# A readiness margin for the TensorE groups of one stage's routing, in a kernel ordered by a list scheduler

## The chip, the core and the metric

The kernel runs on one core of a Trainium2 chip. The core has a matmul engine (TensorE, PE in the profile, with its weight loads as PEld), a vector engine (VectorE, DVE), an activation engine (ScalarE, ACT), GpSimd (POOL) and SyncE (SP), which starts most of the DMAs. Each runs its own stream of instructions in the order in which the program lists them, and they wait for each other through semaphores. The metric is the device time of one execution in microseconds, lower is better.

## What is computed

Two layers over `x` of 8 batches x 2496 rows x 256 columns. The first is a mixing layer in the frequency domain; the second a mixture of 8 experts in which each token goes to one expert of limited capacity.

```python
X = np.fft.rfft(x, axis=1)                    # along the 2496 rows
Yr = Xr @ w_r - Xi @ w_i + b_r                # soft-thresholded by 0.01, as is
Yi = Xr @ w_i + Xi @ w_r + b_i
y = np.fft.irfft(Y, n=x.shape[1], axis=1)     # -> 19968 tokens x 256

logits = y @ w_gate                           # 8 experts, cap = 19968 / 8
order = np.argsort(-flat)                     # greedy: best (token, expert) first,
...                                           # an expert closes when it has cap tokens
h = np.maximum(y[mask] @ w1[e], 0.0)          # 256 -> 1024 -> 256, per expert
out[mask] = h @ w2[e]
```

## The kernel before, in words

**The mixing stage** (`phase_a`, some 550 us) goes through the 8 batches as a pipeline. The transform is split as 39 x 64: a short transform of each chunk of `x` (L1120, or L1124 for the last batches), a pass through DRAM that turns the layout, the 64-point transform (L1186), the product with the mixing weights (L1205, twelve 128x256 matmuls per half), the way back (L1221), DRAM again, and the last short transform (L1252, or L1256 for the later batches), whose result `yst` goes to DRAM. fp32 operands are split into a rounded high part and a rest, and multiplied in several passes; the splits keep VectorE, ScalarE and GpSimd busy (L1005 and L1008, L1195 to L1198, L1211 to L1213). L1275 transposes `yst`, L1279 to L1282 cut the transposed tile in three (`yTh`, `yr`, `yTl`), and L1293 multiplies it with the gate weights for the logits.

**The early routing** concerns the first four batches only (`EB = 4`, `EN = 512`). When their logits are there, `ranges` and then `Router.early` look, for each expert, for 512 tokens that belong to it whatever the other batches bring, so that the experts can start on them. This is a long chain of small steps on VectorE with tiny TensorE groups between them, laid among the products of batches 5 to 7. `ranges` has two groups (a transpose at L440, a broadcast at L448). `bisect` halves a threshold 8 times; each time `count` compares the 128x78 logits with it in four `scalar_tensor_tensor` instructions (L467), packs the counts (L471, L472), adds them over the partitions by two small matmuls (L477, L478), and VectorE takes the next threshold from that (L515 to L517). Then follow L810, two groups at L818, and eight groups at L832, whose ranks ScalarE reads (L838, L839). The weights of the first experts are brought meanwhile (L623, cast by L630 on ScalarE, rest by L631 on VectorE).

**Who sets the order.** Nothing is written in execution order. Every step is a task with an engine, a duration from a table, a position and its dependencies (`Plan.add`), and `Plan.run` is a list scheduler: it keeps a clock for each engine, computes when each task is ready (`rtime`: the latest end of its inputs, plus a latency for another engine), and emits the task that can start first; on TensorE `beside` also chooses among those that are ready by the form of the matmul before. What the planner emits is the order of each engine's stream on the chip. A task that the planner holds for ready later is emitted later, and so stands behind more of the others.

**Three places that the steps below come back to.** The PSUM tiles `pt` (transposes of L1275, groups of L440, L818 and L832) and `pc` (counts) are slices of one bank, which the profile shows under the name `both`:

```python
if self.both is None: self.both = self.pp.tile([128, 512], F32, name="both", tag="both", bufs=1)
n, o = int(np.prod(shape[1:])), 0 if s == "pt0" else 480
```

The planner treats `pt` and `pc` as two buffers. The program that is built treats `both` as one tile: a matmul that writes either slice waits for all earlier readers of both, which are `yTh` on ScalarE (L1279) and `yr` on VectorE (L1280). Second, the products of L1205 write to the ring `ps3` of two banks, so that a product waits until VectorE has read the last but one (L1213). Third, a cast of expert weights (L630) stands in ScalarE's stream and holds what is behind it until the weights have landed.

Of the kernel before, what the change touches and what calls it, by code (L numbers as in the profile page):

```python
# [103 lines left out]
class Plan:  # L104
# [11 lines left out]
        self.bufs.append(b)  # L116
        return b

    def add(self, eng, dur, pos, emit, reads=(), writes=(), tail=0.0, after=(), uses=(), nbytes=0.0, form='r', slack=None):
        t = Task()  # L120
        t.form, t.slack = form, slack
        t.eng, t.dur, t.pos, t.emit, t.tail, t.nbytes = eng, dur, pos, emit, tail, nbytes
        t.deps, t.writes, t.end = set(after), list(writes), None
        for b in reads:
            t.deps.update(b.writers)
        t.ords = set()
        for b in writes:
            if b.state:
                t.ords.update(b.users)
                b.users, b.writers = [], []  # L130
            b.writers.append(t)
        for b in list(reads) + list(writes) + list(uses):
            b.users.append(t)
        t.id = len(self.tasks)
        self.tasks.append(t)
        return t
# [24 lines left out]
    def run(self):  # L161
# [21 lines left out]
        def rtime(t):  # L183
            r = 0.0
            for d in t.deps:
                r = max(r, d.end + (lat if d.eng != t.eng else self.own.get(t.eng, 0.0)))
            for d in t.ords:
                r = max(r, d.end + (lat if d.eng != t.eng else 0.0))
            return r
        for t in self.tasks:  # L190
            if not left[t]:
                ready.setdefault(t.eng, []).append([0.0, t])
# [48 lines left out]
        while n < len(self.tasks):  # L241
            best = None
            for eng, lst in ready.items():
                f = free.get(eng, 0.0)
                cand, hold = [], self.hold.get(eng, 0.0)
                for item in lst:
                    r = slot(item[1], item[0])
# [14 lines left out]
            t = item[1]  # L262
# [21 lines left out]
            for s in succ.get(t, ()):  # L284
                left[s] -= 1
                if not left[s]:
                    ready.setdefault(s.eng, []).append([rtime(s), s])
# [23 lines left out]
class Kit:  # L311
# [29 lines left out]

    def dram(self, kind, shape): return self.plan.buf(kind, lambda s: self.dp.tile(shape, F32, name=s, tag=s, bufs=1))

    extra, both, pace = 0.0, None, None

    def v(self, n, pos, emit, reads, writes): return self.plan.add('V', 0.068 + n / 960 + self.extra, pos, emit, reads, writes, after=self.pace() if self.pace else ())

    def t(self, dur, pos, emit, reads, writes, tail=0.0, form='b', slack=None): return self.plan.add('T', dur, pos, emit, reads, writes, tail=tail, form=form, slack=slack)

    def dma(self, pos, emit, nbytes, reads, writes, **k): return self.plan.add('SP', 0.65, pos, emit, reads, writes, tail=1.9, nbytes=nbytes, **k)  # L350

# [61 lines left out]
def load_logits(K, H, LG, LGb, b, lo, pos):  # L413
    q, h = b // 2, b % 2
    for t, r, n, w in ((H.ML[64 * h:64 * h + 64, :, JP * q:JP * q + JP], 0, 8, H.b_ML), (None, 8, 16, lo)):
        K.dma(pos, lambda t=t, r=r, n=n: K.nc.sync.dma_start(lo.t[64 * h:64 * h + 64] if t is None else t, LG[b, r:r + n].rearrange("v (p j) -> p v j", j=JP)), 80e3, [LGb[b]], [w])
# [895 lines left out]
def fast(tc, nc, H, x, w_r, w_i, b_ri, w_gate, cD1, cF, cG, cD5, YD, LG, w1, w2, cR, out, spectral=True):  # L1312
# [10 lines left out]
    with ExitStack() as ctx:  # L1323
        K = Kit(tc, nc, ctx, RINGS, GROUPS)
        K.plan.add('P', 0.5, -28, lambda: make_identity(nc, H.idn), [], [H.b_idn])
        if spectral:
            YDb, LGb, first, Ft = phase_a(K, H, x, w_r, w_i, b_ri, w_gate, cD1, cF, cG, cD5, YD, LG)
        else:
            first, Ft, YDb, LGb = K.plan.buf(None, None), None, *[[K.plan.buf(None, None) for _ in range(B)] for _ in range(2)]
        pos0 = lambda b: 10 * b + 21  # L1330
        constants(K, H, cR, 11, [first], Pace(K.marks, 11, 21, 10))
        R, X = Router(K, H, None, cR), Experts(K, H, YD, YDb, w1, w2, out)
        for b in range(8):
            if not b % 2: lo = K.sb("lo", [128, 16, JP])
            load_logits(K, H, LG, LGb, b, lo, pos0(b))
            if b % 2 and b < 7: route_prep(K, H, b // 2, lo, lambda b=b: pos0(b) + 1)
            if b == EB - 1:
                ranges(K, H, pos0(b) + 1)
                K.extra = 0.12
                R.early(Pos(52.5, 78, 128), Ft)  # L1340
                K.extra = 0.0
        R.late()
        base = 1000
        jobs = []
        for e in range(8):
            W = X.load(base - 33.623, e=e)
            X.run(EN, base, W, R.egi, 4 * e, R.egs[e], R.eoi, 4 * e, lambda t, base=base: base - 22 + .1 * t, early=True)
            base += 16
        for i in range(8):
            wi, gi, gs, oi = R.closing(i, Pos(1023.987 + 63.312 * i, (1114.017 if i else 1135.422) + 63.312 * i, 211 if i < 2 else 98), lo)  # L1350
            W = X.load(base - 26.393, wi=wi)
            X.run(CAP - EN, base, W, gi, 0, gs, oi, 0, lambda t, base=base: base + 16 * (t // 4) - 8.936 + .1 * (t % 4))
            base += 62
        K.lay(RINGS, [("sh", 20480)] + [(k, 2048) for k in dict.fromkeys(s[:-1] for s in G2)] + [("xTh", 3072), ("xTl", 3072), ("xt", 4096), ("half", 64), ("FG", 16384), ("wt", 4096), ("fg", 4096)])
        K.v(1, 2000, lambda: K.V.tensor_copy(H.fail, R.last[0].t[0:1, 0:1]), [R.last[0]], [H.b_fail])
        return K.plan.run()
# [208 lines left out]
```

## Time and profile before

| what | value |
|---|---|
| time, median of 3 runs | 1544.82 us (1542.28 to 1545.27) |
| the profiled execution | 1553.47 us |
| its span, first to last instruction | 1551.6 us |
| TensorE busy | 1517.0 us, 98% of the span |
| VectorE busy | 1071.9 us, 69% |
| ScalarE busy | 852.4 us, 55% |
| GpSimd busy | 670.9 us, 43% |
| granted TensorE clock, mean | 0.996 |

The profiled execution takes 8.65 us more than the median of the runs; 1.87 us of its time lie outside the span. Busy shares are means over stages that differ: the mixing stage with the early routing in it, and then the experts. A matmul's end is modelled, so gaps between matmuls say more than the busy share does. The early routing stands between about 380 and 545 us of the span.

### The profile page before, as it was taken

How to read it: one execution, taken by the hardware profiler on the slowest of the kernel's cores; microseconds unless marked ns; L12 is line 12 of the kernel's file. 1: busy time of each engine (PE TensorE's matmuls, PEld its weight loads, DVE VectorE, ACT ScalarE, POOL GpSimd, SP SyncE). 2: the span in 40 equal slices, each digit the busy share in tenths (PEclk: the TensorE clock that was granted, in tenths of full speed). 3: DMA queues.
4: the chain of work that ended last, by engine and by line, in shares of the span. 5: the costliest groups of instructions: out<-in, count | busy, mean ns of one | idle time of the engine just before them, and what ended most of it. 6: DMA issues, size and time to landing. Idle time of an engine off the chain costs nothing.

```text
span 1551.6 us, 31427 instructions
## 1 busy us (share of the span) xinstructions
PE 1517.0 (98%) x10927; PEld 1357.1 (87%) x10927; DVE 1071.9 (69%) x3524; ACT 852.4 (55%) x1870; POOL 670.9 (43%) x889
## 2 busy tenths in 40 slices
PE   8999999999899999999999999999999999999998
PEld 6998989998788977888788998998998989989997
DVE  4676667676985674789989989887777765542321
ACT  3777888787668787444636235344343443643332
POOL 2246566574535445343333434434335344343332
PEclk9999999999999999999999999999999999999999
DMA  8787787877768576433213122121211212211110
GB/s 271 228 268 245 229 256 232 253 243 214 229 191 279 155 221 176 150 128 115 89 43 102 47 74 67 47 89 57 96 35 55 88 53 97 96 46 45 43 48 29
DMA packets 143892, 210.58 MB, mean 136 GB/s; under 512 B 27836, under 2 KB 107660, under 8 KB 143724
## 3 DMA queue, kind: packets, MB, share of 16 engines
q1 hardware_dynamic: 126882, 164.59, 34.0%
q0 software_dynamic: 16640, 43.77, 8.9%
q8 instruction: 88, 1.44, 0.4%
q14 instruction: 80, 0.66, 0.1%
q10 hardware_dynamic: 202, 0.12, 0.0%
HBM read 123.67 MB, written 84.49 MB: 134 GB/s over the span
## 4 chain that ended last, share of the span: by engine, by line
PE 80%; DVE 6%; issue 4%; DMA 4%; ACT 3%; POOL 1%; SPq 0%; another core or an unknown queue 0%; POOLq 0%; ACTq 0%; DVEq 0%
PE ps L709 25%; PE ps L683 19%; PE ps L1205 10%; PE p L683 6%; PE ps L1186 4%; PE ps L1221 3%; PE p L1120 3%; PE ps L668 2%; PE p L1252 2%; PE p L1256 2%; DVE junk L467 1%; PE both L1275 1%; DMA sh<-T 1%; ACT ajunk L554 1%; DMA xt<-in_moe_w_dram 1%
## 5 line engine op out<-in xcount | busy, mean ns | idle before, releaser
L1205 PE MATMUL ps<-wt,xTh 128*128 128x256 f32 x1280 | 241.6, 287 | 1.0 <-DVE cnt L472 0.7
L1205 PEld LDWEIGHTS ps<-wt,xTh 128*128 128x128 f32 x1280 | 199.9, 188 | 15.1 <-issue 7.1
L1008 POOL TENSOR_TENSOR zl<-y,zh 128x512 fp32r<-128x512 f32 x80 | 108.1, 1351 | 164.2 <-ACT zh L1005 152.7
L1205 PE MATMUL ps<-wt,xTl 128*128 128x256 f32 x640 | 178.6, 279 | 0.0
L722 POOL DMA_INDIRECT out_dram<-xTh,li x64 | 66.3, 1036 | 248.8 <-ACT xTh L718 206.2
L467 DVE SCALAR_TENSOR_TENSOR junk<-h_m,st,h_AG 128x156 bf16<-128x156 f32 (+1 forms) x472 | 163.2, 390 | 2.6
L1282 POOL TENSOR_TENSOR yTl<-yr,yTh 128x468 bf16<-128x468 f32 (+1 forms) x88 | 98.5, 1120 | 86.2 <-ACT yTh L1281 70.1
L1205 PEld LDWEIGHTS ps<-wt,xTl 128*128 128x128 f32 x640 | 120.1, 188 | 0.0
L722 POOL DMA_INDIRECT out_dram<-xTl,li x64 | 65.2, 1019 | 93.0 <-ACT xTl L718 74.1
L1186 PE MATMUL ps<-FG,sh 128*128 128x128 f32 x640 | 99.2, 280 | 4.9 <-DMA TB<-s4st 3.7
L718 ACT COPY xTl<-ps 128x256 f32<-128x256 f32 x80 | 29.9, 374 | 126.2 <-PE ps L709 94.1
L1186 PEld LDWEIGHTS ps<-FG,sh 128*128 128x128 f32 x640 | 87.6, 194 | 11.3 <-DMA TB<-s4st 3.8
L709 PE MATMUL ps<-FG,yTh 128*128 128x256 f32 x430 | 95.0, 283 | 0.0
L709 PE MATMUL ps<-FG,y 128*128 128x256 f32 x443 | 94.2, 281 | 0.0
L718 ACT COPY xTh<-ps 128x256 f32<-128x256 f32 x72 | 27.0, 374 | 110.9 <-PE ps L709 86.8
L1008 POOL TENSOR_TENSOR s2l<-s2c,s2h 120x512 fp32r<-120x512 f32 (+2 forms) x60 | 76.6, 1279 | 21.5 <-DVE s2h L1005 18.3
L1211 DVE TENSOR_TENSOR ps<-ps,bt 128x512 f32<-128x512 f32 x80 | 55.4, 693 | 34.1 <-PE ps L1205 32.7
L1008 DVE TENSOR_TENSOR xl<-xt,xh 117x512 fp32r<-117x512 f32 (+1 forms) x66 | 56.8, 871 | 31.2 <-ACT xh L1005 30.1
L709 PE MATMUL ps<-FG,s1st 128*128 128x256 f32 x341 | 73.4, 284 | 0.0
L1196 DVE TENSOR_TENSOR xTl<-ps,xTh 128x512 fp32r<-128x512 f32 x80 | 54.7, 683 | 25.2 <-ACT xTh L1195 25.1
L1213 DVE SCALAR_TENSOR_TENSOR y<-ps,y 128x512 f32<-128x512 f32 x80 | 55.0, 688 | 24.6 <-ACT y L1212 23.7
L709 PEld LDWEIGHTS ps<-FG,yTh 128*128 128x128 f32 x430 | 70.6, 188 | 1.6
(757 smaller groups left out, 5084.4 us busy)
## 6 DMA issues: line engine op xcount, KB each, us to landing
xt<-in_moe_w_dram SPq DMA_DIRECT2D x64, 512.0 KB
T<-s4st SPq DMA_DIRECT2D x80, 256.0 KB
s2c<-T SPq DMA_DIRECT2D x80, 240.0 KB
YD<-yst SPq DMA_DIRECT2D x80, 234.0 KB
xt<-in_x_dram SPq DMA_DIRECT2D x35, 512.0 KB
sh<-T SPq DMA_DIRECT2D x35, 512.0 KB
T<-s1st SPq DMA_DIRECT2D x70, 240.0 KB
sh<-in_x_dram SPq DMA_DIRECT2D x5, 512.0 KB
```

Source lines behind the costliest of these rows:

```text
L467: v(cols + 59 + 1400 * K.extra, p, lambda k=k: V.scalar_tensor_tensor(junk[k % 2].t[:, 0:cols], H.m[:, 0:cols], c.t[:, k // ng:k // ng + 1 ...
L683: T.matmul(ps.t[:, 0:w], lhsT=W1.t[:, a, m, 128 * ft:128 * ft + 128], rhs=x_.t[:, 0:w], start=q + m == 0, stop=q + m == 3)
L709: T.matmul(ps.t[0:M], lhsT=a.t[:, 128 * q:128 * q + M], rhs=W2.t[:, w_, ft], start=k == 0, stop=k == 23)
L718: else: plan.add('A', .27, pos + 1, lambda: A.copy(o.t[0:M], ps.t[0:M]), [ps], [o])
L722: ins = P.indirect_dma_start(out=self.out, out_offset=bass.IndirectOffsetOnAxis(ap=oi.t[0:M, oo + t:oo + t + 1], axis=0), in_=o.t[0:M], in ...
L1008: lambda: eng.tensor_tensor(lb[1](), src(), hb[1](), op=OP.subtract), [srcb, hb[0]], [lb[0]])
L1186: T.matmul(ps.t[:, i, 128 * dt:128 * dt + 128], lhsT=sh.t[:, k, 128 * dt:128 * dt + 128], rhs=Ft.t[:, k], start=True, stop=True)
L1196: plan.add('V', dve(512), pos, lambda th=th, tl=tl, src=src, apart=apart: apart(V.tensor_tensor(cols(tl, 64, 192), src(), cols(th, 64, 192 ...
L1205: T.matmul(ps3.t[:, i], lhsT=a.t[:, i, dt, o:o + 128], rhs=wt[c].t[:, w, dt], start=n == 0, stop=n == 11)
L1211: plan.add('V', dve(512), pos + 1.282, lambda ps3=ps3: V.tensor_tensor(ps3.t, ps3.t, bt[:, None, :].to_broadcast([128, 2, 256]), op=OP.add ...
L1213: K.marks[10 * b + p] = plan.add('V', dve(512), pos + 1.282, lambda y=y, ps3=ps3, t=t: V.scalar_tensor_tensor(y.t, ps3.t, 0.0, t.t, op0=OP ...
L1282: yq.append(plan.add('P', pool(2 * W), pos + 0.376, lambda yh=yh, yl=yl, yr=yr, W=W: P.tensor_tensor(yl.t[:, :, 0:W], yr.t[:, :, 0:W], yh. ...
```

## The change

Tasks get a `margin`, 0 for all but the TensorE groups of `ranges` and `Router.early`, where it is 0.7 of the planner's microseconds. `rtime` adds it to the time from which the task counts as ready. No instruction is added or removed on TensorE or VectorE, and no duration in the table is altered; only the planner's order is another one, and with it the choice of some buffers. The line numbers of the changed kernel are one higher from L121 on.

```diff
-    def add(self, eng, dur, pos, emit, ..., form='r', slack=None):
+    def add(self, eng, dur, pos, emit, ..., form='r', slack=None, margin=0.0):
         t = Task()
+        t.margin = margin
...
             for d in t.ords:
                 r = max(r, d.end + (lat if d.eng != t.eng else 0.0))
-            return r
+            return r + t.margin
...
-    extra, both, pace = 0.0, None, None
+    extra, margin, both, pace = 0.0, 0.0, None, None
...
-    def t(self, dur, ...): return self.plan.add('T', dur, ..., slack=slack)
+    def t(self, dur, ...): return self.plan.add('T', dur, ..., slack=slack, margin=self.margin)
...
             if b == EB - 1:
+                K.margin = 0.7
                 ranges(K, H, pos0(b) + 1)
-                K.extra = 0.12
+                K.extra, K.margin = 0.12, 0.7
                 R.early(Pos(52.5, 78, 128), Ft)
-                K.extra = 0.0
+                K.extra, K.margin = 0.0, 0.0
```

The streams are the same up to the broadcast of `ranges` (L448). From there to the end of the mixing stage they differ; from the first count of the later routing on (some 635 us) TensorE's streams run nearly row for row again. Three places:

TensorE before, from the transposes (L1275) to the first count (L477); `both` is the shared bank, `cnt` the packed counts.

```order
L1275 MATMUL both<-h_idn,yst_5886 128x117 x4
L1186 MATMUL ps_5907<-FG_260,sh_5124 128x128 x2
L1120 MATMUL p_5929<-xh_5762,d_94 120x512
L1120 MATMUL p_5929<-xl_5808,d_94 120x512
L1120 MATMUL p_5929<-xh_5762,d_94 120x512
L477 LDWEIGHTS h_ones
L477 MATMUL both<-cnt_5911,h_ones 128x4
```

TensorE of the change, the end of the same stretch: the count (now L478) follows the same transposes, L1186 and L1120 (now L1187 and L1121), and then three matmuls of L1253, the first of which is not shown, and the half of a product.

```order
L1253 MATMUL p_5939<-s2l_5887,d_95 117x512
L1253 MATMUL p_5939<-s2h_5849,d_95 117x512
L1206 MATMUL ps_5950<-wt_342,xTh_5779 128x256 x2
L1206 MATMUL ps_5950<-wt_342,xTl_5828 128x256
L1206 MATMUL ps_5950<-wt_342,xTh_5779 128x256 x2
L1206 MATMUL ps_5950<-wt_342,xTl_5828 128x256
L1206 MATMUL ps_5950<-wt_346,xTh_5779 128x256 x2
L1206 MATMUL ps_5950<-wt_346,xTl_5828 128x256
L1206 MATMUL ps_5950<-wt_346,xTh_5779 128x256 x2
L1206 MATMUL ps_5950<-wt_346,xTl_5828 128x256
L478 LDWEIGHTS h_ones
L478 MATMUL both<-cnt_5932,h_ones 128x4
```

The first count has moved behind three matmuls of the last transform and twelve of a product.

VectorE before, where it frees the bank of a product (L1213 reads `ps_5954`, for which the product `ps_6137` waits); `junk` rows are the compares of the third count.

```order
L467 SCALAR_TENSOR_TENSOR junk_100,acc<-h_m,st_6087,h_AG 128x78
L467 SCALAR_TENSOR_TENSOR junk_101,acc<-h_m,st_6087,h_AG 128x78
L467 SCALAR_TENSOR_TENSOR junk_100,acc<-h_m,st_6087,h_AG 128x78
L467 SCALAR_TENSOR_TENSOR junk_101,acc<-h_m,st_6087,h_AG 128x78
L515 TENSOR_TENSOR cno_6121<-st_6087,h_wk 128x1
L471 TENSOR_SCALAR cnt_6123<-acc 128x4
L1213 SCALAR_TENSOR_TENSOR y_6125<-ps_5954,y_6085 128x512
L472 TENSOR_TENSOR cnt_6123<-acc,cnt_6123 128x4
```

VectorE of the change, where it frees the bank for the same product (L1214 reads `ps_5950`, the last but one there).

```order
L1197 TENSOR_TENSOR xTl_6085<-ps_5912,xTh_6010 128x4x128
L1199 TENSOR_TENSOR xTl_6085<-xTh_6010,ps_5912 128x4x64
L1006 CAST s2h_6102<-s2c_5909 120x512
L517 TENSOR_SCALAR g_6110,any_6111<-both 128x8
L1006 CAST s2h_6114<-s2c_5946 120x512
L518 SCALAR_TENSOR_TENSOR st_6124<-any_6111,h_wk,cno_6059 128x1
L1214 SCALAR_TENSOR_TENSOR y_6128<-ps_5950,y_6104 128x512
L468 SCALAR_TENSOR_TENSOR junk_100,acc<-h_m,st_6124,h_AG 128x78
```

The third count's compares have moved behind L1214, and one L1197, one L1199 and two L1006 have moved ahead of it, counted from the last row that the streams share.

ScalarE before, around the second weight cast of the first expert; `yTh<-both` reads the transposes.

```order
L1257 COPY yst_7326<-p_7299 117x512
L1281 CAST yTh_7304<-yr_7324 128x468
L630 CAST sh_7278<-xt_7258 128x1024
L1279 CAST yTh_7355<-both 128x468
L1005 CAST zh_7360<-y_7331 128x512
```

ScalarE of the change, around both weight casts (now L631; the readings of the transposes are now L1280).

```order
L1224 COPY s4st_7404<-ps_7377 128x512
L1006 CAST zh_7409<-y_7386 128x512
L631 CAST sh_7416<-xt_7296 128x1024
L1280 CAST yTh_7432<-both 128x468
L631 CAST sh_7416<-xt_7333 128x1024
L1301 COPY lgst_7473<-ps_7436 128x234
```

The casts stand later among the products, and each other's neighbours; a reading of the transposes still stands directly behind one.

## Rows read from the trace of the kernel before

**Rows 1.** Busy us by stretch: PE, PEld, DVE, ACT, POOL; clock; DMA share, GB/s.

```profile
380.00:450.00 70.00, 64.04 (x520) 55.59 (x519) 68.04 (x205) 46.65 (x93) 33.94 (x29) 1.00 0.66 204
450.00:550.00 100.00, 98.53 (x794) 83.83 (x793) 60.61 (x116) 82.24 (x213) 47.22 (x50) 1.00 0.68 208
550.00:580.00 30.00, 27.60 (x196) 20.68 (x195) 23.84 (x42) 24.10 (x47) 15.53 (x12) 1.00 0.77 238
580.00:880.00 300.00, 295.57 (x2020) 259.04 (x2019) 244.32 (x1023) 144.60 (x308) 119.30 (x185) 0.99 0.34 109
```

**Rows 2.** TensorE's waits, 380 to 450 us: us in total, times, longest.

```profile
PE both L477 <- DVE yr L1280: 3.1, 3, 1.5
PE both L440 <- DVE yr L1280: 1.4, 1, 1.4
PE ps L1205 <- DVE cnt L472: 0.7, 1, 0.7
PE ps L1205 <- DVE y L1213: 0.3, 1, 0.3
PE ps L1221 <- POOL zl L1008: 0.3, 1, 0.3
```

**Rows 3.** Timeline, first count: start us, us, engine, instruction, [idle before <-releaser].

```profile
395.41 0.15 DVE L472 TENSOR_TENSOR cnt<-acc,cnt 128x4 bf16<-128x4 f32 x1
...
396.08 0.64 DVE L1280 TENSOR_TENSOR yr<-both,yTh 128x468 f32<-128x468 f32 x1
...
396.77 0.16 PE L477 MATMUL both<-cnt,h_ones 128*128 128x4 bf16 x1 [1.53 <-DVE yr L1280]
```

**Rows 4.** Timeline of TensorE and VectorE, second count to third.

```profile
403.32 0.16 PE L477 MATMUL both<-cnt,h_ones 128*128 128x4 bf16 x1 [0.80 <-DVE yr L1280]
...
405.64 0.41 DVE L1005 CAST s2h<-s2c 120x512 fp32r<-120x512 f32 x1
405.97 0.29 DVE L467 SCALAR_TENSOR_TENSOR junk<-h_m,st,h_AG 128x78 bf16<-128x78 f32 x1
...
408.07 0.69 DVE L1213 SCALAR_TENSOR_TENSOR y<-ps,y 128x512 f32<-128x512 f32 x1
...
408.90 0.47 PE L1205 MATMUL ps<-wt,xTh 128*128 128x256 f32 x2 [0.71 <-DVE cnt L472]
409.21 0.28 PE L1205 MATMUL ps<-wt,xTl 128*128 128x256 f32 x1
...
409.29 0.68 DVE L1196 TENSOR_TENSOR xTl<-ps,xTh 128x512 fp32r<-128x512 f32 x1
...
409.33 0.40 PE L1205 MATMUL ps<-wt,xTh 128*128 128x256 f32 x2
...
410.22 2.12 DVE L1005 CAST s2h<-s2c 120x512 fp32r<-120x512 f32 x2
```

**Rows 5.** Timeline, sixth count, directly behind its transposes.

```profile
429.04 0.56 PE L1275 MATMUL both<-h_idn,yst 117*128 117x117 f32 x4
...
430.24 0.16 PE L477 MATMUL both<-cnt,h_ones 128*128 128x4 bf16 x1 [0.18 <-ACT yTh L1279]
```

**Rows 6.** Timeline, expert weights and the transposes behind them.

```profile
483.53 0.38 SPq L623 DMA_DIRECT2D xt<-in_moe_w_dram  x1
...
491.82 1.05 ACT L630 CAST sh<-xt 128x1024 fp32r<-128x1024 f32 x1 [2.35 <-DMA xt<-in_moe_w_dram]
...
494.74 0.62 PE L1275 MATMUL both<-h_idn,yst 117*128 117x117 f32 x4 [1.31 <-DVE yr L1280]
```

**Rows 7.** Timeline, a compare beside GpSimd.

```profile
392.95 0.29 DVE L467 SCALAR_TENSOR_TENSOR junk<-h_m,h_c,h_AG 128x78 bf16<-128x78 f32 x1
393.03 1.34 POOL L1008 TENSOR_TENSOR s2l<-s2c,s2h 120x512 fp32r<-120x512 f32 x1 [0.66 <-DVE junk L467]
...
393.17 1.30 DVE L467 SCALAR_TENSOR_TENSOR junk<-h_m,h_c,h_AG 128x78 bf16<-128x78 f32 x1
```

**Rows 8.** Lines, 380 to 450 us, compares from the second count on: busy us, mean ns | idle.

```profile
L467 DVE SCALAR_TENSOR_TENSOR junk<-h_m,st,h_AG 128x78 bf16<-128x78 f32 x28 | 15.1, 593 | 0.0
```

More of the change, by code (lines that the diff above doesn't have):

```diff
@@ L117, in buf, with add @@
         return b
-    def add(self, eng, dur, pos, emit, reads=(), writes=(), tail=0.0, after=(), uses=(), nbytes=0.0, form='r', slack=None):
+    def add(self, eng, dur, pos, emit, reads=(), writes=(), tail=0.0, after=(), uses=(), nbytes=0.0, form='r', slack=None, margin=0.0):
         t = Task()
+        t.margin = margin
         t.form, t.slack = form, slack
@@ L342, in dram, with t @@
     def dram(self, kind, shape): return self.plan.buf(kind, lambda s: self.dp.tile(shape, F32, name=s, tag=s, bufs=1))
-    extra, both, pace = 0.0, None, None
+    extra, margin, both, pace = 0.0, 0.0, None, None
     def v(self, n, pos, emit, reads, writes): return self.plan.add('V', 0.068 + n / 960 + self.extra, pos, emit, reads, writes, after=self.pace() if self.pace else ())
-    def t(self, dur, pos, emit, reads, writes, tail=0.0, form='b', slack=None): return self.plan.add('T', dur, pos, emit, reads, writes, tail=tail, form=form, slack=slack)
+    def t(self, dur, pos, emit, reads, writes, tail=0.0, form='b', slack=None): return self.plan.add('T', dur, pos, emit, reads, writes, tail=tail, form=form, slack=slack, margin=self.margin)
     def dma(self, pos, emit, nbytes, reads, writes, **k): return self.plan.add('SP', 0.65, pos, emit, reads, writes, tail=1.9, nbytes=nbytes, **k)
```

## Prediction

> **What bounds the kernel now.** The table of part 1 comes first: TensorE is busy for 98% of the span, at a mean granted clock of 0.996. The change adds no work to it, so all that can be won is idle time between matmuls, and only where the order moves. The windows show where that is [rows 1]. From 380 to 450 us TensorE is idle 70 − 64.04 = 5.96 us, and VectorE only 70 − 68.04 = 1.96 us: here VectorE sets the pace. From 450 to 550 us TensorE is idle 1.47 us. The 30 us behind that hold 2.40 us more, at the first experts' start, and the 300 us after it, where the order is nearly the old one, 4.43 us. What the change can touch directly is therefore about 7.4 us, 0.5% of the time; and in the stretch where most of it lies the vector engine has no slack to lose.
>
> The table of waits says what these 5.96 us are [rows 2]. Three counts of the bisection wait 3.1 us for `yr`, the transpose of `ranges` 1.4 us for the same, and two products 1.0 us for VectorE to free their PSUM bank. Behind the first count's wait stands no data that came late: its packed counts were done at 395.41 + 0.15 = 395.56 us; it waited 1.53 us until `yr`, which reads the other slice of the shared bank, was done at 396.72 [rows 3]. The planner doesn't know of that coupling, so it puts the count where its own inputs are ready, and the margin is blind to it too: it moves the count back, whatever that brings.
>
> **The transpose of `ranges`** keeps its place, and its 1.40 us [rows 2] stay: 0.
>
> **The first count.** TensorE was free for it at 396.77 − 1.53 = 395.24 us [rows 3]. In the change three matmuls of L1253 and the twelve 128x256 matmuls of half a product stand ahead as well. Neighbouring products start every 0.12 us per matmul (409.21 to 409.33 [rows 4]), so the twelve alone last 1.44 us, to 396.68, and with the three it is past 396.77. This wait goes, wholly: at most 0.5 us of it could stay, if `yr` were late by as much as the spread of its neighbours.
>
> **Where that time goes.** The saved time is real only as far as the next thing TensorE needs is there. That is the product `ps_6137`. Ahead of it both orders have the same matmuls. It begins at 408.90 us; the row names the short L472 as the releaser, which stands just behind the instruction that the product really needs: L1213, whose `y_6125` reads the bank of the last product but one and ends at 408.07 + 0.69 = 408.76 [rows 4]. Without any wait ahead TensorE would be there at 408.90 − 0.71 − 0.80 − 1.53 = 405.86 us [rows 3, 4], some 3.04 us before its bank is free. The two counts' waits are thus not lost twice: they are taken out of a wait that would stand here anyway.
>
> So the term is how much earlier VectorE gets to this `y`. Counted from the last row that the two orders share, the change takes four compares, L515 and L471 from ahead of it, which last from 405.97 to 408.07 = 2.10 us [rows 4], and puts there one L1197 and one L1199 (409.29 to 410.22 = 0.93 us for these two, under their old numbers) and two casts of L1006 (0.33 us from start to start each, 405.64 to 405.97 [rows 4]): 1.59 us. The `y` comes 0.51 us earlier, at 408.39 with the same 0.14 us to the product, and TensorE idles 408.39 − 405.86 = 2.5 us there in place of 3.04 in three pieces. **Gain 0.5 us.** One of the four compares met GpSimd and took 1.30 us instead of 0.29 (below); whether these instructions meet it in the new order is the uncertainty, 1.01 us each way for each [rows 7], so this term lies between a gain of 1.5 and, with two or three meetings, a loss of 2.6.
>
> **Groups directly behind their transposes.** The sixth count stood so before and waited 0.18 us for ScalarE's reading of the same bank [rows 5]. In the changed order the broadcast and the fourth and fifth counts stand so too. Three times 0.18 is **0.55 us lost**. Below, nothing at all, if ScalarE comes to `yTh` quickly; above, the second count's 0.80 [rows 4] each, 2.4. I take the 0.18, since the pattern is exactly that of its row.
>
> **The fifth count's wait for `yr`**, what is left of the 3.1 us when 1.53 and 0.80 are taken away [rows 2 to 4], goes: **0.75 us gained**. The two waits of 0.3 (a product for `y`, L1221 for GpSimd [rows 2]) don't depend on the counts, and stay.
>
> **The weight cast.** At 494.74 us transposes wait 1.31 us for `yr`. What is late there is ScalarE: its cast waited 2.35 us for weights asked for at 483.53, and the reading of the transposes is queued behind it [rows 6]. In the change the weights are asked for later and the casts stand later, around another reading of the transposes (`yTh_7432`), and one group of L833 reuses that bank behind them. If the weights land in time, 1.31 is won; if both casts wait as this one did, and the bank with them, 1 us more is lost, about the length of the cast itself (1.05 [rows 6]). The casts moved with their loads, so part of the wait should come along: I take **0.6 us gained**, between a gain of 1.31 and a loss of 1.
>
> **The rest.** The stretch from 550 to 580 us and the experts keep their order but for shifts; their 2.40 and 4.43 us [rows 1] wait for the transposes and roundings of their own inputs, which the change neither adds nor takes: 0.
>
> **The sum**: −0.5 + 0.55 − 0.75 − 0.6 = −1.3 us. The profiled execution took 1553.47 us, of which 1.87 lie outside its span; it would take 1552.2. It is 8.65 us above the median of the three runs, a difference in which these waits have no part that I can see, so I put the same 1.3 us against the median: 1544.8 − 1.3 = **1543.5 us**. Measurements of this kernel tell about 0.2%, 3.1 us, from no change.
>
> **The rivals.** (B) *The margin works to the full.* Products find their banks free, since VectorE, no longer held by results that come late, runs ahead; the first two counts' waits, the product's 0.71 and the fifth count's 0.75 all go, 3.79 us, and the weight cast's 1.31, against 0.75 at the groups behind transposes: −4.35, or 1540.5 us. For it: nothing but a table of order stands between. Against it: 1.96 us of idle time on VectorE in 70 [rows 1]; a saturated engine frees no bank earlier because TensorE asks earlier.
>
> (C) *The waits only change places.* What the first count gives back the next product takes, the weight cast waits as before at its new place, and the time is 1544.8, or up to 0.5 either way. For it: the same saturated VectorE, and each moved group still shares its bank.
>
> (D) *Slower: VectorE meets GpSimd more often.* A compare takes 0.29 us alone; one that began at 393.17 beside an L1008 of GpSimd, begun at 393.03, took 1.30, and ended as that did [rows 7]. From 380 to 450 us the 28 compares from the second count on took 15.1 us [rows 8] where 28 x 0.29 would be 8.1: seven meetings or so at 1.01 us each. The change lays all later counts anew against GpSimd's roundings. VectorE has 1.96 us to spare, so it decides from the third additional meeting on; with five more, 5.05 − 1.96 = 3.1 us on the path, and a few tenths more at the groups behind transposes where the gains fail, some 3 to 4.5 us in all: about 1548.5. Against it: with seven meetings in 28 already, a new order is as likely to shed some.
>
> [...]
>
> **How the numbers follow.** My forecast, waits partly traded, 1542 to 1545: 0.45. B: 0.22. C: 0.18. D: 0.15. The range reaches down to B with another meeting fewer, 1539.5, and up to the lower part of D, 1547.0; about 0.1 is left out at each end. Faster by over 0.2% needs 1541.7 or less: most of B and the low edge of the forecast, with a met or missed lock, 0.27. Slower needs 1547.9: most of D, 0.12. The rest, 0.61, is no change that can be told.
>
> **What the profile of the change would show.** Right: the transpose (now L441) still waits about 1.4 us; the first count (L478) has no wait, or under 0.5; a product of L1206 waits 1.5 to 2.6 us around 406 to 408 us, released by VectorE at L1214; the fourth to sixth counts wait 0.1 to 0.4 us each for ScalarE's `yTh`; idle time of TensorE from 380 to 450 us falls from 5.96 to about 5.3; a wait of some 0.7 us is left around 490 to 500. Wrong: no product waits for L1214 (then B); more than 16.5 us in the compares of that window and a VectorE that is busy in nearly all of it up to 455 us (then D); or waits that appear in the experts, where I put nothing.

## The result, and the profile after

The change is slower: 1553.2 us (median of 6 runs, 1550.08 to 1554.36) against 1543.85 us before (6 runs, 1542.21 to 1547.55), a ratio of 1.0053, 95% interval 1.0037 to 1.0068. The prediction was 1543.5 us, with 1539.5 to 1547.0 as its range and 0.12 for slower. Measured again on another chip the ratio was 1.0054 (1.0040 to 1.0069). The level differs from chip to chip: the kernel before had medians of 1544.0 to 1552.5 us on the five chips of the experiments, so all that follows compares runs on one chip. The 8.65 us by which the first profile of before exceeded its median are of that size; where they come from was not shown.

The same views of the change, windows first (columns as in [rows 1]; the short windows are there for the clock, the third column from the right). Then its waits, 380 to 450 us, and single rows of its timeline.

```profile
380.00:450.00 70.00, 64.38 (x512) 56.31 (x510) 63.39 (x188) 46.62 (x92) 34.62 (x29) 0.98 0.65 198
450.00:550.00 100.00, 98.70 (x786) 84.63 (x785) 69.44 (x139) 82.25 (x211) 48.94 (x50) 1.00 0.69 209
550.00:580.00 30.00, 25.92 (x195) 18.80 (x194) 19.66 (x32) 22.01 (x44) 15.74 (x13) 0.94 0.79 249
580.00:880.00 300.00, 294.88 (x1996) 256.98 (x1995) 243.88 (x1007) 145.84 (x310) 115.45 (x183) 0.99 0.34 108
...
408.00:412.00 4.00, 3.12 (x19) 3.15 (x20) 4.00 (x15) 0.64 (x2) 2.63 (x2) 0.75 0.76 226
411.00:412.00 1.00, 1.00 (x7) 1.00 (x6) 1.00 (x6) 0.02 (x1) 0.00 (x0) 0.50 0.44 150
...
412.00:416.00 4.00, 4.00 (x29) 3.79 (x29) 1.89 (x6) 2.94 (x6) 1.08 (x1) 0.83 0.87 294
...
572.00:576.00 4.00, 3.38 (x14) 2.70 (x15) 2.33 (x4) 2.25 (x5) 1.99 (x3) 0.73 0.90 286
576.00:580.00 4.00, 4.00 (x29) 2.77 (x29) 0.69 (x1) 1.30 (x4) 1.81 (x2) 0.85 0.77 229
```

```profile
PE ps L1206 <- DVE y L1214: 1.6, 1, 1.6
PE both L478 <- ACT yTh L1280: 1.4, 2, 1.1
PE both L441 <- DVE yr L1281: 1.4, 1, 1.4
PE ps L1222 <- POOL zl L1009: 0.5, 1, 0.5
PE both L1276 <- ACT yst L1258: 0.4, 1, 0.4
PE both L449 <- ACT yTh L1280: 0.3, 1, 0.3
```

```profile
397.90 0.16 PE L478 MATMUL both<-cnt,h_ones 128*128 128x4 bf16 x1
...
406.70 1.30 DVE L1006 CAST s2h<-s2c 120x512 fp32r<-120x512 f32 x1
...
408.06 0.68 DVE L1214 SCALAR_TENSOR_TENSOR y<-ps,y 128x512 f32<-128x512 f32 x1
...
408.88 0.47 PE L1206 MATMUL ps<-wt,xTh 128*128 128x256 f32 x2 [1.61 <-DVE y L1214]
...
431.29 0.16 PE L478 MATMUL both<-cnt,h_ones 128*128 128x4 bf16 x1 [1.14 <-ACT yTh L1280]
...
552.82 0.32 PE L1276 MATMUL both<-h_idn,yst 117*128 117x117 f32 x1 [1.17 <-ACT yst L1258]
...
572.62 0.32 PE L1276 MATMUL both<-h_idn,yst 117*128 117x117 f32 x1 [1.72 <-DVE yr L1281]
...
852.00 0.33 PE L669 MATMUL ps<-h_idn,s2c 128*128 128x128 f32 x1 [1.96 <-DMA s2c<-YD,li]
```

The reader is to see three things. From 380 to 450 us TensorE idles 5.62 us, hardly less than the 5.96 of [rows 1]: the counts' waits of [rows 2] have become a product's, as forecast. But the idle time is packed: 1.61 us at 408.88 and, just ahead, the 0.5 and 0.4 us of L1222 and L1276; and behind it the mean granted clock is 0.75 and 0.83. These two windows share one stretch at 0.50 (the window from 411 to 412 us lies inside it), and it costs 4 x 0.25 + 4 x 0.17 = 1.7 us of full clock. Last, there are waits where the prediction put nothing: 4.08 us of idle time from 550 to 580 us (2.40 before), with the clock down again behind the 1.72 us (0.73 and 0.85 from 572 to 580 us), and a wait of 1.96 us for gathered tokens at 852 us. The prediction had named waits in the experts as a sign that it was wrong.

Windows of a second trace of the kernel before (b_again below), whose first count also waits 1.5 us (at 396.8 us) and whose product again waits 0.7:

```profile
380.00:450.00 70.00, 64.56 (x523) 56.02 (x523) 68.04 (x205) 46.66 (x93) 33.87 (x29) 1.00 0.66 203
...
396.00:400.00 4.00, 3.24 (x26) 3.09 (x26) 3.72 (x10) 2.89 (x6) 2.12 (x2) 1.00 0.81 229
...
408.00:412.00 4.00, 3.28 (x29) 3.15 (x29) 4.00 (x9) 2.29 (x4) 2.49 (x2) 1.00 0.93 258
...
450.00:550.00 100.00, 100.00 (x811) 85.94 (x811) 62.66 (x120) 84.19 (x217) 48.44 (x51) 1.00 0.69 213
550.00:580.00 30.00, 27.60 (x192) 20.37 (x191) 22.36 (x40) 23.51 (x46) 14.59 (x14) 1.00 0.77 244
```

From 380 to 450 us it idles about as much, 5.44 us, in pieces farther apart, and the clock stays at 1.00.

### The profile page after: what moved, and what is told of

Same layout as the page of the kernel before. It is cut to its first block, busy times and chain, and to the rows that moved or that the text cites. A ratio compares the mean times of both kernels' runs of the same rounds, so it can differ in the third digit from the quotient of the medians.

```text
span 1552.1 us, 31435 instructions
## 1 busy us (share of the span) xinstructions
PE 1517.8 (98%) x10927; PEld 1357.6 (87%) x10927; DVE 1075.1 (69%) x3524; ACT 851.7 (55%) x1870; POOL 668.7 (43%) x889
## 4 chain that ended last, share of the span: by engine, by line
PE 79%; ACT 5%; issue 5%; DVE 5%; DMA 4%; POOL 2%; SPq 0%; POOLq 0%; ACTq 0%; DVEq 0%
PE ps L710 25%; PE ps L684 18%; PE ps L1206 10%; PE p L684 6%; PE ps L1187 4%; PE p L1121 3%; PE ps L1222 3%; PE ps L669 2%; PE p L1253 2%; DMA sh<-T 1%; ACT ajunk L555 1%; PE p L1257 1%; PE both L1276 1%; PE ps L703 1%; POOL out_dram L723 1%
## 5 line engine op out<-in xcount | busy, mean ns | idle before, releaser
L1009 POOL TENSOR_TENSOR zl<-y,zh 128x512 fp32r<-128x512 f32 x80 | 109.6, 1370 | 159.6 <-ACT zh L1006 148.0
L1187 PE MATMUL ps<-FG,sh 128*128 128x128 f32 x640 | 99.3, 280 | 5.2 <-DMA TB<-s4st 3.6
L1187 PEld LDWEIGHTS ps<-FG,sh 128*128 128x128 f32 x640 | 87.4, 194 | 10.7 <-DMA TB<-s4st 3.7
L1009 POOL TENSOR_TENSOR s2l<-s2c,s2h 120x512 fp32r<-120x512 f32 (+2 forms) x60 | 76.8, 1283 | 22.8 <-DVE s2h L1006 20.5
L710 PE MATMUL ps<-FG,y 128*128 128x256 f32 x389 | 86.2, 283 | 0.0
L1009 DVE TENSOR_TENSOR xl<-xt,xh 117x512 fp32r<-117x512 f32 (+1 forms) x66 | 56.2, 862 | 30.8 <-ACT xh L1006 30.5
L710 PE MATMUL ps<-FG,yTl 128*128 128x256 f32 x320 | 75.6, 280 | 0.0
L684 PE MATMUL ps<-yTh,sh 128*128 128x512 f32 (+1 forms) x201 | 73.9, 387 | 0.0
L1197 DVE TENSOR_TENSOR xTl<-ps,xTh 128x512 fp32r<-128x512 f32 x80 | 54.6, 683 | 26.9 <-ACT xTh L1196 26.9
```

The lines of the kernel that those rows point to most:

```text
L684: T.matmul(ps.t[:, 0:w], lhsT=W1.t[:, a, m, 128 * ft:128 * ft + 128], rhs=x_.t[:, 0:w], start=q + m == 0, stop=q + m == 3)
L710: T.matmul(ps.t[0:M], lhsT=a.t[:, 128 * q:128 * q + M], rhs=W2.t[:, w_, ft], start=k == 0, stop=k == 23)
L1009: lambda: eng.tensor_tensor(lb[1](), src(), hb[1](), op=OP.subtract), [srcb, hb[0]], [lb[0]])
L1187: T.matmul(ps.t[:, i, 128 * dt:128 * dt + 128], lhsT=sh.t[:, k, 128 * dt:128 * dt + 128], rhs=Ft.t[:, k], start=True, stop=True)
L1197: plan.add('V', dve(512), pos, lambda th=th, tl=tl, src=src, apart=apart: apart(V.tensor_tensor(cols(tl, 64, 192), src(), cols(th, 64, 192 ...
```

## The experiments

Each timed run lists its span and its mean granted clock. So for every kernel the mean of (1 − clock) x span says what a lower clock took, counted as if TensorE had work throughout, and the mean of clock x span what the rest took. The table gives both as differences to the runs of before on the same chip, in us; the first row, before against itself, shows the scatter, about 1 us. Where a run's planner has added code, its line numbers are higher than in the two kernels: the count L477 is L508 in one_move, for example. Edits that name tasks by number are given in words.

| run | ratio to before (95%) | by the clock | the rest |
|---|---|---|---|
| b_again (before, unchanged) | 0.9996 (0.9986 to 1.0006) | −1.2 | +0.1 |
| after_again (the change) | 1.0054 (1.0040 to 1.0069) | +5.6 | +3.9 |
| mix_early | 1.0041 (1.0028 to 1.0054) | +2.8 | +3.7 |
| mix_late | 1.0008 (0.9997 to 1.0018) | −0.6 | +1.8 |
| early_only | 0.9987 (0.9975 to 0.9998) | +0.1 | −1.4 |
| ranges_only | 1.0003 (0.9992 to 1.0014) | +0.2 | +0.3 |
| margin_half | 1.0046 (1.0028 to 1.0064) | +3.4 | +4.1 |
| one_move | 1.0016 (1.0004 to 1.0028) | +2.8 | −0.7 |
| mix_routing | 1.0061 (1.0040 to 1.0081) | +5.1 | +4.3 |
| mix_tail | 1.0047 (1.0033 to 1.0060) | +4.0 | +3.4 |
| fix_tail | 1.0082 (1.0061 to 1.0103) | +4.0 | +7.6 |
| fix_counts | 1.0068 (1.0050 to 1.0087) | +5.8 | +3.9 |
| fix_both | 1.0065 (1.0043 to 1.0087) | +1.9 | +7.8 |
| coupled | 0.9987 (0.9975 to 1.0000) | +1.1 | −3.5 |
| coupled_2 (the same again) | 0.9988 (0.9973 to 1.0003) | +0.2 | −2.8 |
| coupled_margin | 1.0048 (1.0030 to 1.0066) | +4.3 | +3.4 |
| coupled_late | 0.9988 (0.9974 to 1.0002) | +0.7 | −2.6 |
| coupled_early | 0.9995 (0.9982 to 1.0008) | +1.0 | −1.9 |

**Where in the span.** b_again is the kernel before, unaltered. In the two others the planner runs twice without emitting, with and without the margin, and then emits a joined order. At its task 3300 (about 580 us) both orders have emitted the same set.

```diff
+        order = moved[:3300] + plain[3300:]           # mix_early
+        order = plain[:3300] + moved[3300:]           # mix_late
```

> The kernel before, unchanged, for a second profile and a floor: its only profiled execution took 1553.5 us, while its timed runs have a median of 1543.9. Both theories: 1544 us, ratio 1.000 within 0.002. What a typical execution does not have of the first profile should show: I expect the 3.3 us wait at the closing's L549 near 1360 us and the stretches of half clock near 745 and 1362 us to be smaller or gone.

> The planner's order with the margin for its first 3300 tasks (up to about 580 us of the span), then the order without it. At task 3300 both orders have emitted exactly the same set. Theory A (the loss is made among the products: the product's 1.6 us wait, the 1.1 and 1.7 us waits of 552 and 572 us, and the lower clock behind them): 1550 to 1554 us, as the change. Theory B (the loss is made among the experts, where the order and the choice of buffers are also new): 1543 to 1546 us, as before.

> The reverse: the order without the margin for the first 3300 tasks, then the order with it. Theory A: 1543 to 1546 us, as before. Theory B (a new order of the experts' stage between about 700 and 850 us, and other buffers from 580 us on): 1550 to 1554 us.

The unchanged kernel kept its 3.2 us wait at L549 in the second trace, with a mean granted clock of 0.82 and 0.75 in the two 4 us windows from 1356 to 1364 us, against what I expected; the low clock near 745 us (0.57 from 744 to 748 us in the first trace) was gone (1.00). Theory A holds for most of the loss: mix_early has 6.5 of the change's 8 to 9.5 us, mix_late a small part, not clear of no change in its ratio. In the trace of mix_late the wait for gathered tokens is the only long one that before lacks:

```profile
847.97 0.44 PE L696 MATMUL ps<-h_idn,s2l 128*128 128x128 f32 x2 [1.38 <-DMA s2l<-YD,li]
```

**Which margin.** Each of the two settings alone, half of both, and the whole change once more.

```diff
-                K.margin = 0.7
+                K.margin = 0.0                        # early_only
-                K.extra, K.margin = 0.12, 0.7
+                K.extra, K.margin = 0.12, 0.0         # ranges_only
+                K.margin = 0.35 ... 0.12, 0.35        # margin_half
```

> The margin for the groups of Router.early alone, not for the two of ranges. Against the kernel before only 143 rows of TensorE differ, all between the second count and the last ranks; buffers and the experts' order are those of before. Theory A: most of the loss, since nine of ten groups with a margin are kept: 1548 to 1553 us. Theory B: 1543 to 1546 us.

> The margin for the two groups of ranges alone. The run with the margin in Router.early alone was not slower. Theory that one of the two parts carries the cost: as the change, 1.004 to 1.006 of before. Rival, that any new order of this stretch is a draw (the broadcast's move reorders all behind it, the experts too, and differently from the change): anything between 0.997 and 1.006, with its own long waits and its own stretches of lower clock, which explain it place by place.

> Margin 0.35 in place of 0.7. The streams are those of the change up to the fourth count and from the experts' start; between about 415 and 480 us 268 rows of TensorE stand otherwise. If the change's cost were in proportion to the margin: half of it, 1.0025. If it is a matter of places: the product's wait of 1.6 us at 408 us and those at 552 and 572 us stay, with the lower clock behind them, and only the sixth count's 1.1 us can go: 1.003 to 1.005.

> The change unaltered, beside the kernel before on one chip. By the runs so far (mix_early lost 2.8 us by a lower clock and 3.7 us at full clock, mix_late 1.8 us at full clock and none by the clock): about 8 us slower, ratio 1.005, of which 2 to 4 us by the clock and 4 to 6 us idle, and the trace with the waits near 408, 431, 552, 572 and 852 us again. Rival, that the loss is the clock's alone: 7 to 8 us by the clock, nothing at full clock.

Neither margin costs anything alone, both together cost 0.54%, and halves of both nearly as much. For early_only, theory A had expected most of the loss. So the cost is neither in proportion to a margin nor that of one of them; this fits the rival of ranges_only, that each new order is a draw, whose wide range could hardly have failed. margin_half did not keep the product's 1.6 us wait, as I had expected it to: the product waits 0.71 us, as before, and the clock does not fall there (1.00 from 408 to 416 us). It falls behind another wait:

```profile
409.63 0.36 PE L1206 MATMUL ps<-wt,xTh 128*128 128x256 f32 x1 [0.71 <-DVE cnt L473]
...
570.30 0.46 PE L1276 MATMUL both<-h_idn,yst 117*128 117x117 f32 x1 [1.69 <-DVE yr L1281]
```

```profile
572.00:576.00 4.00, 4.00 (x11) 3.13 (x10) 1.11 (x2) 0.94 (x2) 2.15 (x4) 0.50 0.91 231
```

So the loss does not hang on the place at 408 us alone. The change's own runs lose more by the clock than by the rest: each of the six of after_again loses 10.9 us or more by it, none of the 17 of before more than 9.3. Its second trace has the low clock at other places: behind the 1.6 and the 1.1 us wait, and not behind the 1.7 us at 573:

```profile
408.00:412.00 4.00, 4.00 (x24) 4.00 (x24) 2.76 (x12) 0.77 (x2) 2.12 (x3) 0.61 0.73 175
...
432.00:436.00 4.00, 4.00 (x24) 4.00 (x24) 2.73 (x13) 0.94 (x2) 1.13 (x2) 0.62 0.24 73
572.00:576.00 4.00, 2.92 (x16) 2.40 (x17) 2.42 (x4) 2.71 (x6) 2.12 (x3) 1.00 0.89 279
```

These places recur in the traces of the runs, so the cases can be counted. Behind the wait of 1.6 us near 408 us the clock falls in six of the seven traces that have it (0.61 to 0.80 from 408 to 412 us; 1.00 in mix_routing), behind the one of 1.7 us near 572 us in six of seven (0.50 to 0.73 in the lowest 4 us window; 1.00 in after_again), behind the fifth count's 1.1 us in three of seven (0.61 to 0.64 from 432 to 436 us; 1.00 in the others), and behind the first count's 1.5 us of the old order in none of four (1.00 from 396 to 400 us). The length of a wait alone does not decide it: in the trace of early_only the clock falls behind two waits of 0.74 and 0.93 us, 1.7 us apart.

```profile
407.49 0.49 PE L1253 MATMUL p<-s2l,d 120*117 120x512 f32 x1 [0.74 <-POOL s2l L1009]
...
409.15 0.55 PE L1206 MATMUL ps<-wt,xTh 128*128 128x256 f32 x1 [0.93 <-DVE cnt L473]
```

```profile
408.00:412.00 4.00, 3.07 (x14) 2.88 (x14) 4.00 (x10) 1.74 (x3) 2.21 (x2) 0.63 0.88 250
```

**One move alone.** The order before, with only the first count put behind the twelve matmuls.

```diff
+        t, after = (first count), (second half of that product)
+        order = [u for u in plain if u is not t]
+        order.insert(order.index(after), t)
```

> The order before, with one move alone: the first count stands behind the twelve matmuls of a product's half, as in the change. Theory of the traded wait (as predicted): the count's 1.53 us wait goes, and a product of L1205 near 408 us waits for L1213 instead of 0.7 us some 2 us; nothing else changes, so 0 to 1 us either way. Theory of the clock (the runs so far): the same idle time in one piece lets the granted clock fall behind it, which the change's traces show at 408 us, for some 1.7 us more: 1 to 2 us slower, and a stretch near 408 us at a granted clock below 0.8. If the move wins the whole wait: 1.5 us faster.

This is the cleanest of the runs. About a dozen instructions of TensorE stand otherwise, a handful of VectorE, and none of ScalarE and GpSimd. The first count's wait is gone and so is the product's, and, against the expectation, it is the second count that waits in their place:

```profile
401.95 0.16 PE L508 MATMUL both<-cnt,h_ones 128*128 128x4 bf16 x1 [2.17 <-DVE yr L1311]
```

```profile
400.00:404.00 4.00, 2.05 (x7) 1.60 (x7) 4.00 (x16) 1.41 (x3) 1.08 (x1) 0.70 0.41 131
404.00:408.00 4.00, 4.00 (x25) 3.29 (x24) 3.77 (x16) 2.81 (x6) 1.28 (x1) 0.87 0.72 206
...
380.00:450.00 70.00, 65.29 (x522) 57.18 (x520) 68.00 (x204) 46.25 (x92) 33.72 (x28) 0.98 0.67 205
```

TensorE idles 4.71 us in the stretch, less than any trace of before (5.44 and 5.96). The rest of the time falls by some 0.7 us, no more than the scatter, and yet the kernel is slower, by 2.8 us of clock: ten of its twelve runs lose over 7 us by the clock, one of the 29 of before does. What its trace shows for it is one wait of 2.17 us in place of 1.5 and 0.8 apart, with 4 x 0.30 + 4 x 0.13 = 1.7 us of clock behind it; where the other 1.1 us are lost is not shown.

**One place at a time.** Two more joined orders, at a task where the sets differ, and single groups mended within the change's order.

```diff
+        order = moved[:2950], then the rest as in plain            # mix_routing
+        order = plain[:2950], moved up to 3300, then plain         # mix_tail
+        order = moved, second of two transposes behind two L684 groups, its logits later   # fix_tail
+        order = moved, first count back, another count two L1120 later   # fix_counts; fix_both: all
```

> The order of the change for the planner's first 2950 tasks (up to about 545 us of the span), then whatever is left in the order without the margin. It keeps the change's 1.6 us wait of a product at 408 us and the sixth count's 1.1 us, and gives the batch 7 transposes between 550 and 580 us their old places. If each place carries its own cost: no 1.2 and 1.7 us waits at 552 and 572 us and no low clock at 574 us, 1.0015 to 1.003 of before. Rival, that the waits at 552 and 572 us follow from what the routing did before: they stay, 1.004 to 1.005.

> The reverse: the order before for the first 2950 tasks, the order of the change up to task 3300 (about 580 us), then the order before. If each place carries its own cost: before's waits up to 545 us, the 1.2 and 1.7 us waits at 552 and 572 us with the clock behind the latter; 1.0015 to 1.003 of before. Rival: 1.000.

> The change's order with one place mended: the second of two transposes in a row at 572 us, and the logits' product behind it, stand behind the expert matmuls that follow them; 23 rows of TensorE. Theory of the places: the 1.7 us wait goes and with it the low clock at 572 to 580 us (1.7 us), 3 us won of the change's 8: 1.003 to 1.0035 of before. Rival, the order as a whole: the wait reappears at the next transposes, 1.005.

> The change's order with the other two places mended: the first count back at its place of before, the sixth behind two more matmuls of L1120. Theory of the places: the first count waits 1.5 us again, the product at 408 us only the rest (under 0.8), the sixth count under 0.5, so idle time falls by some 0.7 us and the clock no longer falls behind them: 2 to 3 us won, 1.003 to 1.004 of before. Rival: 1.005, with the product's wait as it was.

> Both mends together. Theory of the places: both gains, 5 to 6 us won, 1.001 to 1.002 of before; what is left is the experts' other order (1.0008 in its own run) and the wait of 1.2 us at 552 us. Rival: 1.004 to 1.005.

The two joined orders settle nothing of the sizes. Each made a wait of its own at the seam (the first row is of mix_routing, the second of mix_tail):

```profile
558.04 0.47 PE L1234 MATMUL ps<-wt,xTh 128*128 128x256 f32 x2 [3.00 <-DVE gm L604]
```

```profile
552.28 0.65 PE L1304 MATMUL both<-h_idn,yst 117*128 117x117 f32 x2 [2.47 <-ACT yst L1286]
```

The mends won nothing either. In fix_tail the 1.72 us came back as four waits of 2.5 us together, though the clock stayed at 1.00 there; why the rest of its time is 7.6 us longer than before's, twice the change's, stays open:

```profile
572.45 0.51 PE L714 MATMUL ps<-s2l,sh 128*128 128x512 f32 x1 [0.97 <-ACT s2l L702]
573.32 0.50 PE L714 MATMUL ps<-s1st,sh 128*128 128x512 f32 x1 [0.36 <-DVE s1st L703]
...
576.93 0.50 PE L714 MATMUL ps<-s1st,sh 128*128 128x512 f32 x1 [0.62 <-DVE s1st L703]
...
578.88 0.69 PE L1287 MATMUL p<-s2c,s2h 120*117 120x512 f32 x1 [0.51 <-DMA s2c<-T]
```

In fix_counts the first count, back at its place, waits 0.79 us, and the product waits its 1.62 as before the mend, so this wait is VectorE's doing and no leftover of the first count's:

```profile
394.71 0.18 PE L508 MATMUL both<-cnt,h_ones 128*128 128x4 bf16 x1 [0.79 <-DVE cnt L503]
...
406.71 0.36 PE L1236 MATMUL ps<-wt,xTh 128*128 128x256 f32 x1 [1.62 <-DVE y L1244]
...
429.12 0.16 PE L508 MATMUL both<-cnt,h_ones 128*128 128x4 bf16 x1 [1.13 <-ACT yTh L1310]
```

The last row corrects the expectations: the wait of 1.1 us belongs to the fifth count, which the expectations call the sixth, and the count that was moved is the seventh. So that place was never mended, and fix_counts and fix_both say nothing of it. That the loss is a sum of places which can be won back one by one was thus not shown: where a mend did reach its place, the wait turned up again near by.

**Telling the planner of the bank.** Counts and transposes use one kind of buffer, so that the planner itself holds a count until `yr` and `yTh` are read.

```diff
-    ps = K.psum("pc", [128, 3])
+    ps = K.psum("pt", [128, 3])
-        th = self.th = bisect(..., ag, C, "pc", self.junk, self.acc)
+        th = self.th = bisect(..., ag, C, "pt", self.junk, self.acc)
-        ps2 = K.psum("pc", [128, 16])
+        ps2 = K.psum("pt", [128, 16])
```

> The kernel before, no margin, but the planner is told that counts and transposes share one bank (both use the kind pt). Theory that the waits come from the planner's blindness to the bank: the three counts' waits for yr go, idle time of TensorE from 380 to 450 us falls from 6 to under 3.5 us, and the time by 2 to 3 us, ratio 0.998. Rival, VectorE sets the pace there: the waits only move to the products, idle time stays at 5 to 6 us, ratio 1.000, or above where a wait is long enough for the clock to fall.

> The coupled kernel without margin once more, beside the others of this call, for a narrower interval: 0.9985 to 0.999 of before by what its trace lost of idle time between 380 and 450 us (2.8 us in place of 5.2); 1.000 if the first measurement was a draw of the clock.

> The change's margin, with the planner told that counts and transposes share one bank. If the margin's harm is that it is laid on a ready time that is itself wrong, it is harmless here: 0.997 to 1.000 of before. If a margin harms by itself (it holds results back that VectorE then has late, and packs waits together), it is slower than the coupled kernel without margin by 2 to 6 us: 1.001 to 1.003.

> The coupled kernel without margin, with the transpose of ranges behind eight more matmuls (L1221 and L1120). Its wait of 1.0 to 1.5 us for yr goes; if VectorE makes up for the later start of the bisection, 1 us is won beside the coupled kernel, 0.998 of before; if the counts behind it wait instead, 0.9985 to 1.000.

> The planner knows of the shared bank, and the margin stands in Router.early alone. If the two gains add up: 0.9975 of before. If a margin on top of a ready time that is now right only holds results back: 1.000 to 1.004, with waits packed together behind the counts. The order is a new one from the third count on, the experts' too, so a draw in either direction is possible.

coupled and coupled_2 are this edit of the kernel before, coupled_margin the same edit of the change. coupled_late also puts the transpose of `ranges` behind eight more matmuls, and coupled_early has the margin in `Router.early` alone. Without a margin the coupled kernel's idle time in this stretch is half of before's, 70 − 67.43 = 2.57 us, and its longest wait but for L440's is 0.7 us:

```profile
380.00:450.00 70.00, 67.43 (x551) 59.60 (x550) 62.50 (x196) 49.10 (x99) 35.60 (x31) 1.00 0.71 216
```

It is the version that points below both kernels: 0.13% and 0.12% faster than before on two chips, each at the edge of its interval, so not clear of no change, with 3.5 and 2.8 us less of the rest; early_only comes out as low. With the margin it is as slow as the change, with new long waits at a count (1.7 us), at L833 (1.5) and at transposes (1.7):

```profile
411.40 0.16 PE L478 MATMUL both<-cnt,h_ones 128*128 128x4 bf16 x1 [1.72 <-DVE yr L1281]
```

That a margin harms only because the ready time is wrong is thereby refuted. The two small gains don't add up in coupled_early, and moving the transpose of `ranges` back won nothing beyond coupled.

## Why the prediction was wrong

**The transpose of `ranges` and the first count: right.** L441 waits 1.4 us; L478 at 397.90 has no wait.

**Where that time goes: the idle time was right, the place nearly.** Predicted were 2.5 us at the product; measured are 1.61 there and 0.5 and 0.4 at L1222 and L1276 just ahead, some 2.5 together. That the sum agrees is in part luck: the `y` that frees the bank came no earlier than before (408.06 against 408.07 [rows 4]). One of the two casts put ahead of it took 1.30 us, beside an L1009 of GpSimd that began at 406.45 and took 1.27, in place of the 0.33 I had priced; a meeting with GpSimd was named as this term's uncertainty.

**What the same idle time costs in one piece: the step that failed first.** The working added and subtracted waits as if a microsecond of idle time cost a microsecond wherever it stands. It named the mean clock of 0.996 and priced nothing of it. one_move shows the price by one move: 0.7 us of the rest won, 2.8 us of clock lost. In the change's own runs it is 5.6 of some 9.5 us. In these traces, where the clock fell behind a wait of 1.1 to 2.2 us, the lowest 4 us window behind it has a mean granted clock of 0.50 to 0.77, and one such wait was enough: in one_move the two windows that hold the 2.17 us and what follows have 0.70 and 0.87. The clock should have been a rival on the slower side; the prediction had only VectorE's meetings with GpSimd there.

**Groups behind their transposes, and the fifth count: mis-sized.** The broadcast and the fourth count wait 0.29 us each, the fifth 1.14, the sixth not at all: 1.72 us for the three times 0.18 on top of the sixth's 0.18. So the 0.75 us that the fifth count's wait for `yr` was to give back came back as 1.14 for `yTh`. The pattern in the order was that of its row, but not ScalarE's queue: its reading of the fifth count's transposes began at 430.68 us, behind an L1213 of 0.69 us and an L1141 of 0.58 us.

**The weight cast: nothing was there to win.** The 1.31 us of [rows 6] are absent in the second trace of the kernel before, whose TensorE has no idle time from 450 to 550 us; in the change it idles 1.30 us there, in waits of 0.4 us and less. A wait that hangs on the landing of a DMA was taken from a single execution.

**"The rest: 0": failed.** I read the order behind 550 us as the old one but for shifts. It was not: batch 7's transposes stand closer together, with 4.08 us of idle time for 2.40, and between some 700 and 850 us the experts' groups are permuted and use other buffers; by mix_late that is worth about 1.8 us, with the 1.4 to 2.0 us wait for gathered tokens as its visible part. The windows of that stretch in the two traces of before, then of the change:

```profile
700.00:880.00 180.00, 176.97 (x1212) 157.94 (x1211) 162.50 (x747) 81.29 (x195) 66.00 (x106) 0.99 0.25 81
700.00:880.00 180.00, 176.80 (x1212) 157.70 (x1211) 163.27 (x754) 79.47 (x194) 69.56 (x112) 1.00 0.25 82
...
700.00:880.00 180.00, 174.88 (x1187) 155.36 (x1186) 160.91 (x734) 80.65 (x194) 62.33 (x104) 0.99 0.24 80
700.00:880.00 180.00, 175.50 (x1187) 155.51 (x1186) 162.30 (x739) 81.43 (x195) 63.97 (x106) 0.99 0.26 84
```

TensorE idles 5.12 and 4.50 us there in place of 3.03 and 3.20. With the 1.7 us from 550 to 580 us that is 3.0 to 3.8 us, most of the 3.9 by which the rest of the change's time grew; from 380 to 450 us the idle time did not grow. By the timed runs the earlier part is the larger one, 3.7 us in mix_early for 1.8 in mix_late; with a scatter of about 1 us the division stays open.

**The rivals.** B's sum takes 0.75 us for the groups behind their transposes where the forecast takes 0.55; nothing hangs on that difference. B did not happen, though its ground was sounder than I allowed: coupled shows that VectorE, which I called saturated, lets TensorE's idle time fall to 2.6 us while itself busy for 62.5 of 70 us. D did not happen: the 28 compares took 14.6 us in the change, not over 16.5, and VectorE is busy for 63.39 us in place of 68.04. C's mechanism did, waits that change places, but with a price. The chance of a faster kernel speaks of a met or missed lock; no run shows a lock. What the traces show is single VectorE instructions that take longer beside a GpSimd one and end close to its end: the compare of [rows 7], and in the change one of 1.30 us at 409.66, beside an L1009 that began at 409.52 and took 1.35 us.

What stays open is why the low clock follows a wait in one execution and not in the next (573 us above), and so how the loss divides over the single places.

## What to carry to other kernels

TensorE's idle time was not additive here (one_move: 0.7 us of the rest won, 2.8 us of clock lost): before moving work so that two short waits become one, look in narrow windows at the granted clock behind waits of that size. When a planner's order is disturbed, price the whole stretch behind the disturbance down to the last row that differs, for this list scheduler answered a small margin with another order everywhere, and two margins that cost nothing apart cost 0.5% together. A cause that the planner doesn't know (a bank shared by two of its buffers) is better told to it than covered by a margin: here telling it took 2.8 to 3.5 us off the rest, though the whole time is not clearly shorter.

## What the runs showed of the hardware that was not expected

A wait of 1.1 to 2.2 us was followed in some of the traces by a stretch at a granted clock of 0.50 (the window from 411 to 412 us of the change). Counted as (1 − clock) over the 4 us windows, it cost about 1.7 us each time, in margin_half 3.4. It followed the waits of 1.6 and 1.7 us near 408 and 572 us in twelve of fourteen cases, the fifth count's 1.1 us in three of seven, and neither the 1.7 us of coupled_margin's count (1.00 from 408 to 416 us) nor, in four traces, the first count's 1.5 us in the order of before. The same program differs by up to 0.55% between chips (medians of 1544.0 and 1552.5 us), as much as the change's whole effect; each chip was measured at one time only.
